# Attention, routed experts and a dense layer in one kernel: VectorE scans ahead of the masks, routing chains in turn, masks made on chip

## The chip, the cores and the metric

The kernel runs on one core of one Trainium2 chip. The metric is the device time of one execution in microseconds; the median of several runs counts. The engines are PE (TensorE), DVE (VectorE), ACT (ScalarE), POOL (GpSimd) and SP, which here only issues transfers.

## What is computed

The reference chains three parts. The shapes are batch 4, 8 heads, 768 steps, head dimension 48, so 3072 tokens of 384 numbers; 8 experts of width 1024; a dense layer of width 2048.

```python
for t in range(S):                                   # attention with decay
    state = alpha[:, :, t, :, None] * state + einsum('bhd,bhe->bhde', k[:, :, t], v[:, :, t])
    y[:, :, t] = einsum('bhd,bhde->bhe', q[:, :, t], state)
xn = x / (norm(x) + 1e-06)                           # routing, one expert per token
en = expert_emb / (norm(expert_emb) + 1e-06)
logits = xn @ en.T / tau
expert_idx = argmax(logits, axis=1)
gate_w = softmax(logits)[expert_idx]
out[mask_e] = gate_w * (maximum(x[mask_e] @ w1[e], 0) @ w2[e])
h = x @ w_in                                         # dense layer
out = where(h > 0, h, exp(minimum(h, 0)) - 1) @ w_out
```

## The kernel before

**Attention** works on 24 tiles of 128 tokens: 6 chunks of time (`cc`), and in each the 4 batch entries, whose state goes from chunk to chunk. `stR` and `stA` are DVE scans over the decays of a tile (`at`): R (L341) and its reciprocal (L342) scale the keys, A (L351) the queries; the products Kh (L344) and Qh (L353) are made on POOL. On PE, `stS` (L381) multiplies Qh by Kh into `psS`; `stP` (L388, DVE, two halves) multiplies that by a triangular mask from `cs` into P; `stC_values` (L426) multiplies P by the values; `stC_state` (L408) adds the part of the old state, from the second chunk on; `stD` (L464) turns a finished tile around and gives its eight logits, which DVE sums into `lg` (L469). `stT` makes the transposed keys and `stC_values` also the new state (U, L434). Three PSUM banks (`psG`) are used in turn: two for the halves of `psS`, one for U. The four `at` and four `qk` buffers are used in turn, with loads issued four tiles ahead on SP. The heads have 48 rows, laid at partitions 0 to 47 and 64 to 111; the rows between them are zeros that the loads of the first four tiles bring along.

The loop in `fast()` runs all engines by the order in which the code stands: pass `i` issues S of tile `i+1`, the scans of tile `i+2`, P of tile `i+1` and then D of tile `i-1` and the values of tile `i`. On DVE a pass is R(i+2), reciprocal, P(i+1) first half, A(i+2), P(i+1) second half, `lg`, then whatever the list `todo` holds.

`todo` is the **routing** of a group of tiles (groups of 6, 6, 4, 4, 2 and 2; the last ones are routed behind the loop). When the group's last tile is `j`, pass `j+2` appends `stR1` (an argmax chain over `lg` and a chain, `inv_norm`, for the norms of the tokens; the second one is a Newton iteration where each step needs the one before), `step` takes up to 12 operations from the list in a pass, pass `j+3` puts `stR2` (the positions of the tokens) ahead of what is left, and pass `j+4` ends the chain and releases the gates. Tokens are then written to DRAM sorted by expert (`put`, with a one-element POOL memset `tick` at L583 ahead of its indirect store). Expert weights come 12 pieces at a time from pass `WAIT-2` on, and each piece is split into a high part on ACT and a low part `wlo` on DVE (L204).

Before the loop the constants `cs` (identity, triangular mask, tables), the embeddings `emb_t` and the selector `rhsX` are loaded; 20 matmuls on `ones16` (`warm`, L285) run on PE, then 4 more behind S of tile 0. The eight embedding rows are normed by a chain of 14 small ACT operations (`inv_norm1`, L140 to L148) that begins and ends with a DVE reciprocal (L732), scaled on ACT (L733, L734), and transposed on PE (`eT`, L762) into the last columns of `rhsX`.

**moe1** goes through the eight experts with three matmuls per product (high by high, high by low, low by high). Beside it `decode` unpacks the dense layer's weights, and the rows of the next expert are loaded (`load_x`) and transposed (`turn`). At its end, `split_x` makes the high and low parts `xh`, `xl` (L1106, L1107) of the first 512 tokens of the dense layer, between the three copies of the last expert's result (L1041, L1042, L1045).

**moe2** has 6 blocks of 512 tokens with 16 steps each: 96 times `mm1` (L1187, nine matmuls into one PSUM bank) and, three steps behind, `mm2` (L1208 to L1210). The result of `mm1` goes through `mn` (L1189, DVE), an exponential (ACT), `g` (L1193, DVE), `gh` (ACT) and `gl` (L1197, DVE); `g` is the last reader of the bank. `mm1` has four banks of its own (`psH2`). In the first block the dense weights are split on the way (`split_dense`, L259 and L260).

Of the kernel before, what the change touches and what calls it, by code (L numbers as in the profile page):

```python
# [22 lines left out]
NT = NC * B  # L23
# [17 lines left out]
WAIT = 10  # L41
# [18 lines left out]
CONST = [("ident", 128), ("tri", 128), ("dec", E), ("base", E), ("tok", NT), ("key", E), ("cap", E), ("iota", E)]  # L60
# [3 lines left out]
def fused_kernel(ctx, tc, qk, a, v, emb, w12, wi, wo, cst, sel, cols, out):  # L64
# [12 lines left out]
    c = {}  # L77
# [25 lines left out]
    ss = const.tile([128, NT], F32, name="ss")  # L103
    tick = const.tile([1, 1], F32, name="tick")
# [23 lines left out]

    def inv_norm1(pool, x):

        shape = [x.shape[0], 1]
        y = pool.tile(shape, F32, name="rs_y1")
        t = pool.tile(shape, F32, name="rs_t1")
        h = pool.tile(shape, F32, name="rs_h1")
        yi, vec, act = y.bitcast(I32), nc.vector, nc.scalar
        first = [
            lambda: vec.tensor_scalar(yi, x.bitcast(I32), 1, None, op0=ALU.logical_shift_right),
            lambda: vec.tensor_scalar(yi, yi, -1.0, float(0x5F3759DF), op0=ALU.mult, op1=ALU.add),
        ]
        steps = [lambda: act.activation(out=h, in_=x, func=AF.Copy, scale=-0.5)]  # L140
        for _ in range(3):
            steps += [
                lambda: act.activation(out=t, in_=y, func=AF.Copy, scale=h),
                lambda: act.activation(out=t, in_=t, func=AF.Copy, scale=y),
                lambda: act.activation(out=t, in_=t, func=AF.Copy, bias=1.5),
                lambda: act.activation(out=y, in_=t, func=AF.Copy, scale=y),
            ]
        steps += [lambda: act.activation(out=y, in_=y, func=AF.Copy, scale=x, bias=1e-6)]  # L148
        return y, first, steps
# [137 lines left out]
    def attention():  # L287
        with ExitStack() as st:
# [27 lines left out]
            def load(i):  # L316
                if i >= NT:
                    return
                cc, b = divmod(i, B)
                at[i], qkt[i] = ats[i % LB], qks[i % LB]  # L320
                for t, src in ((at[i], a), (qkt[i], qk)):
                    for r in [slice(0, C2)] if i < LB else [slice(0, D), slice(HP, C2)]:
                        nc.sync.dma_start(out=t[r], in_=src[cc, r, b])
# [171 lines left out]
            def stR1(g):  # L495
# [168 lines left out]
            def fast():  # L664
                warm_t = sm.tile([128, 1], F32, bufs=1, name="warm_t")
                emb_t = sm.tile([E, 2 * NP * HP + 1], F32, bufs=1, name="emb_t")
# [10 lines left out]
                nc.vector.memset(ones16, 1.0)  # L677
# [5 lines left out]
                for t in G:  # L683
                    nc.gpsimd.memset(t, 0.0)
# [3 lines left out]
                nc.gpsimd.memset(zero, 0.0)  # L688
# [4 lines left out]
                for j in range(2):  # L693
# [3 lines left out]
                    if j == 0:  # L697
                        stE(j)
                        nc.scalar.activation(out=esq, in_=rows, func=AF.Square, accum_out=es)
# [3 lines left out]
                for f in guess:  # L703
                    f()
# [632 lines left out]
```

## Time and profile before

| what | us |
|---|---|
| median of 3 runs (790.78 to 794.12) | 793.1 |
| profiled execution | 795.59 |
| its span | 793.8 |
| attention in the span | 0 to 157 |
| moe1 | 157 to 385.5 |
| moe2 | 386.4 to 793.8 |
| PE busy in the span | 770.1 (97%) |
| DVE busy | 522.2 (66%) |
| ACT busy | 362.6 (46%) |
| POOL busy | 188.9 (24%) |

The stages were told apart by the first and the last matmul of each. The profiled execution is the one whose trace is read below; what lies outside its span is 1.8 us. The mean granted clock of PE over the span is 0.992 of full speed. In a timeline row the first number is the start and the second the duration; a number in square brackets is how long the engine stood idle just before, and behind the arrow is what it was waiting for. A row that ends in x4 is four operations in a row, and its duration runs from the first start to the last end.

### The profile page before, as it was taken

The numbers are of one execution on the slowest core, as the hardware profiler recorded it, in microseconds if no ns is written. First come the engines' busy times: TensorE is split into PE (matmuls) and PEld (weight loads), VectorE is DVE, ScalarE is ACT, GpSimd is POOL, SyncE is SP. The second block draws the span as 40 slices with busy tenths as digits, with TensorE's granted clock in tenths as the row PEclk, the third lists the DMA queues.
The fourth block names the chain that finished last, engine by engine and source line by source line (L and its number), as shares of the span: only waits on it lengthen the run. The fifth ranks groups of instructions, "written<-read, shape, count | busy, mean of one in ns | idle before, by whom it ended". The sixth has DMA issues, their size and how long they took to land.

```text
span 793.8 us, 13698 instructions
## 1 busy us (share of the span) xinstructions
PE 770.1 (97%) x5077; PEld 699.1 (88%) x5077; DVE 522.2 (66%) x1001; ACT 362.6 (46%) x802; POOL 188.9 (24%) x222
## 2 busy tenths in 40 slices
PE   7999998899999999999999999999999999999996
PEld 4888887489999999999898899999999999999996
DVE  6789999846877877896576755454555545545442
ACT  4667877435455455554545433333333323323231
POOL 5545667322333433342000020020002002002002
PEclk9899999999999999999999999999999999999999
DMA  9998773366665666661000010010001001001001
GB/s 245 245 259 205 233 202 92 109 176 201 185 198 184 204 198 204 213 200 35 1 1 1 1 40 1 0 40 1 1 1 40 1 1 40 1 0 41 1 1 40
DMA packets 44804, 76.25 MB, mean 96 GB/s; under 512 B 11958, under 2 KB 21302, under 8 KB 44734
## 3 DMA queue, kind: packets, MB, share of 16 engines
q1 hardware_dynamic: 41662, 65.89, 29.5%
q0 software_dynamic: 3072, 9.45, 3.3%
q8 instruction: 40, 0.66, 0.4%
q14 instruction: 30, 0.25, 0.1%
HBM read 63.12 MB, written 12.22 MB: 95 GB/s over the span
## 4 chain that ended last, share of the span: by engine, by line
PE 40%; issue 30%; DVE 3%; POOL 3%; ACT 2%; POOLq 0%; ACTq 0%
PE h L1187 6%; PE y L1031 5%; PE y L1033 4%; PE y L1032 4%; PE h L1000 4%; PE h L1001 4%; PE h L999 4%; POOL out_dram L1221 2%; PE o L1210 2%; PE o L1208 2%; PE o L1209 2%; PE t L980 1%; DVE dlo L260 1%; DVE g L1193 1%; DVE mn L1189 1%
## 5 line engine op out<-in xcount | busy, mean ns | idle before, releaser
L1189 DVE TENSOR_SCALAR mn<-h 128x512 f32<-128x512 f32 x96 | 66.2, 690 | 139.7 <-PE h L1187 139.7
L1190 ACT ACTIVATE mn<-mn 128x512 f32<-128x512 f32 x96 | 60.7, 632 | 171.7 <-DVE mn L1189 163.2
L1210 PE MATMUL o<-dwo,gl 128*128 128x384 f32 x384 | 129.4, 337 | 1.4 <-DVE gl L1197 1.4
L1209 PE MATMUL o<-dlo,gh 128*128 128x384 f32 x384 | 128.4, 334 | 0.0
L1208 PE MATMUL o<-dwo,gh 128*128 128x384 f32 x384 | 128.2, 334 | 0.0
L1187 PE MATMUL h<-xh,dwi 128*128 128x512 f32 x288 | 112.8, 392 | 0.6 <-ACT x2T L1045 0.6
L1187 PE MATMUL h<-xh,dlo 128*128 128x512 f32 x288 | 113.2, 393 | 0.0
L1187 PE MATMUL h<-xl,dwi 128*128 128x512 f32 x288 | 112.5, 392 | 0.0
L1221 POOL DMA_INDIRECT out_dram<-ob,ids x24 | 23.2, 965 | 340.8 <-ACT ob L1218 337.1
L1196 ACT ACTIVATE gh<-g 128x512 fp32r<-128x512 f32 x96 | 60.7, 633 | 77.9 <-DVE g L1193 77.9
L1003 ACT ACTIVATE hh<-h 128x432 fp32r<-128x432 f32 (+6 forms) x64 | 32.4, 506 | 107.1 <-PE h L1001 98.9
L204 DVE TENSOR_TENSOR wlo<-raw,whi 128x512 fp32r<-128x512 f32 x96 | 72.8, 786 | 5.6 <-ACT whi L201 5.6
L1193 DVE SCALAR_TENSOR_TENSOR g<-mn,h 128x512 f32<-128x512 f32 x96 | 66.1, 688 | 15.2 <-ACT mn L1190 14.7
L1208 PEld LDWEIGHTS o<-dwo,gh 128*128 128x128 f32 x384 | 72.0, 187 | 4.2
L1209 PEld LDWEIGHTS o<-dlo,gh 128*128 128x128 f32 x384 | 72.0, 187 | 4.0
L1210 PEld LDWEIGHTS o<-dwo,gl 128*128 128x128 f32 x384 | 72.2, 188 | 2.1 <-DVE gl L1197 1.7
L1004 DVE SCALAR_TENSOR_TENSOR hl<-h,hh 128x432 fp32r<-128x432 f32 (+6 forms) x64 | 36.7, 574 | 48.8 <-ACT hh L1003 47.4
L1031 PE MATMUL y<-hh,whi 128*128 128x432 f32 (+6 forms) x192 | 68.3, 356 | 0.0
L999 PE MATMUL h<-xh,whi 128*128 128x432 f32 (+6 forms) x192 | 66.5, 346 | 0.7 <-ACTq L1058 0.7
L244 POOL TENSOR_SCALAR dg<-dg 128x384 f32<-128x384 f32 x32 | 41.7, 1304 | 106.3 <-ACT dg L243 106.1
L1197 DVE TENSOR_TENSOR gl<-g,gh 128x512 fp32r<-128x512 f32 x96 | 65.7, 684 | 1.2 <-ACT gh L1196 1.1
L1001 PE MATMUL h<-xh,wlo 128*128 128x432 f32 (+6 forms) x192 | 66.4, 346 | 0.0
(217 smaller groups left out, 1508.9 us busy)
## 6 DMA issues: line engine op xcount, KB each, us to landing
raw<-in_w_dram SPq DMA_DIRECT2D x96, 256.0 KB
qk<-in_qk_dram SPq DMA_DIRECT2D x40, 192.0 KB
raw<-in_wi_dram SPq DMA_DIRECT2D x16, 384.0 KB
raw<-in_wo_dram SPq DMA_DIRECT2D x16, 384.0 KB
vt<-in_v_dram SPq DMA_DIRECT2D x24, 192.0 KB
xr<-xs SPq DMA_DIRECT2D x7, 576.0 KB
at<-in_alpha_dram SPq DMA_DIRECT2D x40, 99.0 KB
xs<-zero SPq DMA_DIRECT2D x7, 288.8 KB
```

The source lines that it names most:

```text
L204: nc.vector.tensor_tensor(l[:, sl], r, h[:, sl].bitcast(F32), op=ALU.subtract)
L999: nc.tensor.matmul(ps, wh, xh[:, kk], start=(kk == 0), stop=False)
L1001: nc.tensor.matmul(ps, wl, xh[:, kk], start=False, stop=(kk == KD - 1))
L1031: nc.tensor.matmul(acc[e][d], wh, hh, start=(f == 0), stop=False)
L1187: nc.tensor.matmul(ps, l, x, start=(n == 0), stop=(n == len(terms) - 1))
L1189: nc.vector.tensor_scalar(mn, ps, 0.0, None, op0=ALU.min)
L1190: nc.scalar.activation(out=mn, in_=mn, func=AF.Exp)
L1193: nc.vector.scalar_tensor_tensor(g, mn, -1.0, ps, op0=ALU.add, op1=ALU.max)
L1197: low.append(lambda: nc.vector.tensor_tensor(gl, g, gh.bitcast(F32), op=ALU.subtract))
L1208: nc.tensor.matmul(o_, gh[:, sl], wh, start=(f == 0), stop=False)
L1209: nc.tensor.matmul(o_, gh[:, sl], wl, start=False, stop=False)
L1210: nc.tensor.matmul(o_, gl[:, sl], wh, start=False, stop=(f == M - 1))
```

## The change

**Start.** The embeddings come within `cs`, unscaled and already in the layout of `rhsX`, so the loads of `emb_t` and `rhsX` and the chain `inv_norm1` with its scaling and its transposes are gone. Identity and triangular mask are made by POOL (`affine_select`) in a tile `masks`; `cs` has 97 columns where it had 320. The zero rows of the first four `qk` tiles are set by DVE and POOL instead of loaded, and the order of the loads is another one; the load of the lower rows waits for the setting. The memsets of G and `zero` on POOL go behind Qh of tile 1. `warm` runs 6 instead of 4 behind S of tile 0, and 3 at the end of pass 0. The norm of the embeddings is a matmul with ones in pass 2 and 17 DVE operations in passes 5 to 7, and one more operation of the routing chain multiplies the logits by it (another is joined to its neighbour, so the count stays).

**DVE order.** `stA` goes ahead of both halves of `stP` in every pass. The two chains of `stR1` alternate one by one, `stR2` alternates with what is left, 16 operations are taken in a pass instead of 12, and a group ends one pass earlier. `WAIT` is 9.

**moe1.** The rows of expert 1 are loaded ahead of two loads of the dense weights, `decode` runs by another schedule of about the same length, and the first `split_x` moves ahead of the last `mm2`.

**moe2.** `mm1` uses the three banks of `psG`, which moe1 used, instead of four of its own, and the special order of terms in the first step is gone.

```diff
-WAIT = 10
+WAIT = 9
...
-CONST = [("ident", 128), ("tri", 128), ("dec", E), ("base", E), ("tok", NT), ("key", E), ("cap", E), ("iota", E)]
+CONST = [("emb", NP * E), ("dec", E), ("base", E), ("tok", NT), ("key", E), ("cap", E), ("iota", E), ("tau", 1)]
...
+            def load_k(i, apart=False):
...
+                for n in [slice(1, 2), slice(0, 1)] if apart else [slice(0, 2)]:
+                    for r in [slice(HP, C2), slice(0, D)]:
+                        nc.sync.dma_start(out=t[r, n], in_=qk[cc, r, b, n])
...
                 ops = [
+                    lambda: nc.vector.tensor_tensor(l, l, en.to_broadcast(s3), op=ALU.mult),
                     lambda: nc.vector.tensor_reduce(mx, l, axis=AX.X, op=ALU.max),
-                    lambda: nc.vector.tensor_tensor(e_, l, mx.to_broadcast(s3), op=ALU.is_equal),
                     lambda: nc.vector.tensor_tensor(l, l, mx.to_broadcast(s3), op=ALU.subtract),
-                    lambda: nc.vector.tensor_tensor(e_, e_, c["dec"][:, None, :].to_broadcast(s3), op=ALU.mult),
+                    lambda: nc.vector.scalar_tensor_tensor(e_, l, 0.0, c["dec"][:, None, :].to_broadcast(s3), op0=ALU.is_ge, op1=ALU.mult),
...
-                load(0)
+                nc.vector.memset(qks[0][lanes, 1], 0.0)
+                nc.vector.memset(ones16, 1.0)
+                nc.vector.memset(qks[0][lanes, 0], 0.0)
+                nc.gpsimd.memset(c["ident"], 0.0)
+                nc.gpsimd.affine_select(out=c["ident"], in_=c["ident"], compare_op=ALU.not_equal, fill=1.0, base=0, pattern=[[-1, 128]], channel_multiplier=1)
+                nc.gpsimd.memset(c["tri"], 1.0)
+                nc.gpsimd.affine_select(out=c["tri"], in_=c["tri"], compare_op=ALU.is_ge, fill=0.0, base=0, pattern=[[1, 128]], channel_multiplier=-1)
+                nc.vector.memset(qks[1][lanes], 0.0)
+                nc.gpsimd.memset(qks[2][lanes], 0.0)
+                nc.gpsimd.memset(qks[3][lanes], 0.0)
+                load(0, True)
+                load(1)
+                load_a(2)
+                load_v(0)
+                load_k(2)
                 nc.sync.dma_start(out=cs, in_=cst)
-                nc.sync.dma_start(out=emb_t, in_=emb)
-                load(1)
-                load_v(0)
-                load(2)
-                nc.sync.dma_start(out=rhsX, in_=sel[:, None, :].to_broadcast([128, NP, CW + E]))
                 load_v(1)
                 load(3)
                 load_v(2)
...
                     stR(i + 2)
+                    stA(i + 2)
                     stP(i + 1, 0)
-                    if i == 0:
-                        nc.vector.reciprocal(en, en)
-                        nc.scalar.activation(out=rows, in_=rows, func=AF.Copy, scale=en)
-                        nc.scalar.activation(out=rows, in_=rows, func=AF.Copy, scale=rtau)
-                    stA(i + 2)
                     stP(i + 1, 1)
...
-                        todo[:0] = stR2(last[i - 3])
+                        todo[:] = in_turn(stR2(last[i - 3]), todo)
...
-                        m, n = stR1(last[i - 2])
-                        k = len(m) // 2
-                        todo.extend([f for x in zip(m[::2], m[1::2], n[:k]) for f in x] + n[k:])
+                        todo.extend(in_turn(*stR1(last[i - 2])))
...
-                    step(5)
+                    step(8 if i < 7 else 16)
                     for f in lag:
                         f()
                     lag.clear()
-                    step(7)
...
-                    for g in [g for j, g in last.items() if i == j + 4]:
+                    for g in [g for j, g in last.items() if i == j + 3]:
...
+            def in_turn(*chains):
+
+                return [x[n] for n in range(max(map(len, chains))) for x in chains if n < len(x)]
...
+                    if n == len(blocks):
...
+                        for kk in range(KD):
+                            split_x(x2T, *first, 0, kk)
                     if n >= LAG:
                         mm2(*blocks[n - LAG])
...
-                    j = (n - 2) * 4 // 7
+                    j = (n - 4) * 3 // 5
...
-                ps = psH.tile([128, U], F32, name="h2")
+                ps = psG.tile([128, U], F32, tag="g", name="h2")
```

DVE behind the first scans, where S of tile 0 has been multiplied: first as it stands in the kernel before, then as it stands now (`rs_y` is the result of the embeddings' norm chain on ACT).

```order
L388 TENSOR_TENSOR P<-psS,cs 128x512 x2
L341 SCALAR_TENSOR_TENSOR R<-at_124,pz 112x528
L342 RECIPROCAL at_124<-R 112x4
L388 TENSOR_TENSOR P<-psS,cs 128x512
L732 RECIPROCAL rs_y_202<-rs_y_202 8x1
L351 SCALAR_TENSOR_TENSOR A<-at_124,pz 112x528
L388 TENSOR_TENSOR P<-psS,cs 128x512
L341 SCALAR_TENSOR_TENSOR R<-at_125,pz 112x528
```

```order
L381 TENSOR_TENSOR P<-psS,masks 128x512 x2
L334 SCALAR_TENSOR_TENSOR R<-at_126,pz 112x528
L335 RECIPROCAL at_126<-R 112x4
L344 SCALAR_TENSOR_TENSOR A<-at_126,pz 112x528
L381 TENSOR_TENSOR P<-psS,masks 128x512 x2
L334 SCALAR_TENSOR_TENSOR R<-at_127,pz 112x528
```

The scan A of tile 2 no longer stands behind the reciprocal of the embeddings' norm, nor behind P of tile 1.

DVE in the second of the passes that route group 0, from P up to the next scan R; before, then now (L561 to L563 and L554 to L556 are `stR2`, L118 to L124 and L120 to L127 the norm chain).

```order
L388 TENSOR_TENSOR P<-psS,cs 128x512
L561 TENSOR_TENSOR t<-psR,oh 128x48
L562 TENSOR_REDUCE pos<-t 128x6
L563 TENSOR_SCALAR pos_i<-pos 128x6
L120 SCALAR_TENSOR_TENSOR rs_y<-rs_t,rs_y 128x6
L118 SCALAR_TENSOR_TENSOR rs_t<-rs_y,ss 128x6
L119 TENSOR_TENSOR rs_t<-rs_t,rs_y 128x6
L120 SCALAR_TENSOR_TENSOR rs_y<-rs_t,rs_y 128x6
L118 SCALAR_TENSOR_TENSOR rs_t<-rs_y,ss 128x6
L119 TENSOR_TENSOR rs_t<-rs_t,rs_y 128x6
L120 SCALAR_TENSOR_TENSOR rs_y<-rs_t,rs_y 128x6
L123 TENSOR_TENSOR rs_y<-rs_y,ss 128x6
```

```order
L381 TENSOR_TENSOR P<-psS,masks 128x512 x2
L554 TENSOR_TENSOR t<-psR,oh 128x48
L122 SCALAR_TENSOR_TENSOR rs_y<-rs_t,rs_y 128x6
L555 TENSOR_REDUCE pos<-t 128x6
L120 SCALAR_TENSOR_TENSOR rs_t<-rs_y,ss 128x6
L556 TENSOR_SCALAR pos_i<-pos 128x6
L121 TENSOR_TENSOR rs_t<-rs_t,rs_y 128x6
L122 SCALAR_TENSOR_TENSOR rs_y<-rs_t,rs_y 128x6
L125 TENSOR_TENSOR rs_y<-rs_y,ss 128x6
L126 TENSOR_SCALAR rs_y<-rs_y 128x6
L127 RECIPROCAL rs_y<-rs_y 128x6
L511 TENSOR_TENSOR lg<-lg,rs_y 128x48
```

The three operations of `stR2` now alternate with the norm chain, which ends in this pass.

ACT from the end of moe1 into moe2; before, then now (L1041, L1045 and L1038, L1040 copy the last expert's result, L1106 and L1103 are the high parts of the first 512 tokens).

```order
L1041 ACTIVATE x2T<-y_7921 128x368
L1106 ACTIVATE xh_8126<-x2T 128x512
L1045 ISA
L1045 ACTIVATE x2T<-y_7923 128x368
L1106 ACTIVATE xh_8127<-x2T 128x512
L1106 ACTIVATE xh_8128<-x2T 128x512
L259 ACTIVATE dwi<-wd 128x384
```

```order
L1103 ACTIVATE xh_8117<-x2T 128x512
L1103 ACTIVATE xh_8118<-x2T 128x512
L1103 ACTIVATE xh_8119<-x2T 128x512
L1035 TENSOR_LOAD off_i
L1035 ISA x2
L1038 ISA
L1038 ACTIVATE x2T<-y_7946 128x368
```

The three high parts go from between and behind the last copies to ahead of them.

## Rows read from the trace of the kernel before

**Rows 1.** Windows: stretch, length, busy PE, PEld, DVE, ACT, POOL; granted clock, DMA share, GB/s
```profile
15.00:20.00 5.00, 2.76 (x22) 2.45 (x23) 3.40 (x6) 2.54 (x7) 2.56 (x2) 0.72 1.08 234
20.00:25.00 5.00, 5.00 (x50) 4.76 (x50) 3.53 (x5) 2.48 (x7) 2.56 (x2) 0.59 1.04 225
35.00:127.00 92.00, 89.22 (x1304) 78.88 (x1300) 84.04 (x190) 68.59 (x217) 53.61 (x54) 1.00 0.78 211
127.00:157.00 30.00, 24.29 (x211) 17.15 (x211) 26.52 (x146) 16.12 (x53) 15.23 (x28) 0.94 0.35 107
200.00:370.00 170.00, 170.00 (x944) 165.16 (x943) 138.13 (x231) 88.66 (x179) 64.38 (x56) 1.00 0.60 189
```

**Rows 2.** Timeline of PE, 8 to 30 us: start, us, line, operation, idle before it
```profile
9.98 1.03 PE L285 MATMUL warm<-ones 128*128 128x512 bf16 x4
...
14.15 0.61 PE L434 MATMUL psU<-vt,Kt 128*64 128x48 f32 x16
16.71 0.41 PE L762 MATMUL eT<-cs,emb_t 8*128 8x8 f32 x4 [1.95 <-ACT emb_t L734]
17.65 2.08 PE L381 MATMUL psS<-Qh,Kh 48*128 48x128 f32 x16 [0.53 <-POOL Qh L353]
...
24.61 1.16 PE L381 MATMUL psS<-Qh,Kh 48*128 48x128 f32 x16
...
29.07 1.16 PE L381 MATMUL psS<-Qh,Kh 48*128 48x128 f32 x16 [0.41 <-POOL Qh L353]
```

**Rows 3.** Timeline of DVE, 10 to 18 us
```profile
14.90 0.15 DVE L732 RECIPROCAL rs_y<-rs_y 8x1 f32<-8x1 f32 x1 [1.42 <-ACT rs_y L148]
```

**Rows 4.** DMA issues from 0 to 12 us: KB each
```profile
qk<-in_qk_dram SPq DMA_DIRECT2D x4, 448.0 KB
...
rhsX<-in_sel_dram SPq DMA_DIRECT2D x1, 208.0 KB
...
cs<-in_cst_dram SPq DMA_DIRECT2D x1, 160.0 KB
```

**Rows 5.** Timeline of POOL, 0 to 7 us
```profile
0.83 1.05 POOL L684 MEMSET G<- 112x256 f32 x4 [0.38 <-POOLq L1325]
...
5.87 1.28 POOL L344 TENSOR_TENSOR Kh<-qk,R 112x512 f32<-112x512 f32 x1 [3.42 <-DMA qk<-in_qk_dram]
```

**Rows 6.** Page, costliest groups: a POOL operation, mean ns of one
```profile
L244 POOL TENSOR_SCALAR dg<-dg 128x384 f32<-128x384 f32 x32 | 41.7, 1304 | 106.3 <-ACT dg L243 106.1
```

**Rows 7.** Timeline of DVE in a plain tile, 45.3 to 51 us
```profile
45.38 0.69 DVE L388 TENSOR_TENSOR P<-psS,cs 128x512 f32<-128x512 f32 x1 [1.43 <-PE psS L381]
45.99 1.24 DVE L351 TENSOR_TENSOR_SCAN A<-at,pz 112x528 f32<-112x528 f32 x1
...
47.83 1.24 DVE L341 TENSOR_TENSOR_SCAN R<-at,pz 112x528 f32<-112x528 f32 x1
...
50.72 0.69 DVE L388 TENSOR_TENSOR P<-psS,cs 128x512 f32<-128x512 f32 x1 [1.43 <-PE psS L381]
```

**Rows 8.** Timeline of DVE in two routing tiles, 50.7 to 63 us
```profile
54.03 0.21 DVE L510 TENSOR_TENSOR lg<-lg,mx 128x48 f32<-128x48 f32 x1
54.15 0.20 DVE L511 TENSOR_TENSOR e__829<-e__829,cs 128x48 f32<-128x48 f32 x1
...
60.09 0.17 DVE L118 SCALAR_TENSOR_TENSOR rs_t<-rs_y,ss 128x6 f32<-128x6 f32 x1
60.30 0.17 DVE L119 TENSOR_TENSOR rs_t<-rs_t,rs_y 128x6 f32<-128x6 f32 x1
```

**Rows 9.** Timeline of PE, 93 to 102 us
```profile
100.00 1.16 PE L381 MATMUL psS<-Qh,Kh 48*128 48x128 f32 x16 [1.26 <-POOL tick L583]
```

**Rows 10.** Timeline of PE at the start of moe2, 386 to 388 us
```profile
386.39 0.50 PE L1187 MATMUL h<-xh,dwi 128*128 128x512 f32 x1 [0.59 <-ACT x2T L1045]
```

**Rows 11.** Timelines of DVE and PE in moe2, 429.5 to 432.5 us
```profile
430.17 0.69 DVE L1193 SCALAR_TENSOR_TENSOR g<-mn,h 128x512 f32<-128x512 f32 x1 [0.16 <-ACT mn L1190]
...
431.91 0.39 PE L1187 MATMUL h<-xh,dwi 128*128 128x512 f32 x1
```

More of the change, by code (lines that the diff above doesn't have):

```diff
@@ L127, in inv_norm @@
         return y, steps
[L129 to L149, printed above, removed]
     wq = [(e, s) for e in range(E) for s in range(FB * FW // SLOT)]
@@ L687, in fast @@
                 zero = xp.tile([128, 1, XW], F32, tag="xt", name="zero")
-                nc.gpsimd.memset(zero, 0.0)
-                rows, rtau = emb_t[:, :2 * NP * HP], emb_t[:, 2 * NP * HP:]
-                es = sm.tile([E, 1], F32, name="es")
-                esq = wk.tile([E, 2 * NP * HP], BF16, bufs=1, tag="junk", name="esq")
-                en, guess, newton = inv_norm1(sm, es)
                 for j in range(2):
@@ L696, in fast @@
                     stH(j)
-                    if j == 0:
-                        stE(j)
-                        nc.scalar.activation(out=esq, in_=rows, func=AF.Square, accum_out=es)
+                    stE(j)
+                for t in G:
+                    nc.gpsimd.memset(t, 0.0)
+                nc.gpsimd.memset(zero, 0.0)
+                nc.gpsimd.memset(ones_f, 1.0)
                 stS(0)
                 stT(0)
-                warm(ps1, "psY", 4)
-                for f in guess:
-                    f()
-                nc.vector.reciprocal(rtau, rtau)
-                stE(1)
+                warm(ps1, "psY", 6)
+                for h2 in range(2):
+                    nc.scalar.activation(out=rhsX[:, :, h2 * D:(h2 + 1) * D],
+                                         in_=c["ident"][:, None, h2 * HP:h2 * HP + D].to_broadcast([128, NP, D]), func=AF.Copy)
                 stP(0, 0)
                 stP(0, 1)
-                for f in newton:
-                    f()
+                inv, norms = inv_norm(sm, es)
+                norms += [
+                    lambda: nc.vector.reciprocal(c["tau"], c["tau"]),
+                    lambda: nc.vector.tensor_tensor(en[:, 0], inv, c["tau"].to_broadcast([128, E]), op=ALU.mult),
+                ]
                 lag = []
@@ L759, in fast @@
                     if i == 0:
-                        eT = psD.tile([128, NP, E], F32, tag="psX", name="eT")
-                        for p in range(NP):
-                            nc.tensor.transpose(eT[:, p], rows[:, p * 128:(p + 1) * 128], c["ident"][:E, :E])
-                        nc.scalar.activation(out=rhsX[:, :, CW:CW + E], in_=eT, func=AF.Copy)
+                        warm(psD, "psX", 3)
+                        nc.scalar.activation(out=rhsX[:, :, CW:CW + E], in_=c["emb"].rearrange("p (n e) -> p n e", n=NP), func=AF.Copy)
+                    if i == 2:
+                        nc.scalar.activation(out=esq, in_=rhsX[:, :, CW:CW + E], func=AF.Square)
+                        nc.tensor.matmul(pz[:, 64:64 + NP * E], ones_f, esq.rearrange("p n e -> p (n e)"), start=True, stop=True)
+                        sums = pz[:, 64:64 + NP * E].rearrange("p (n e) -> p e n", n=NP)
                     if i == 3:
@@ L1084, in moe1 @@
                             turn(e + 1, f - 4)
+                    if n == len(blocks):
+                        for nm in ("xh2", "xl2"):
+                            first.append([stage.tile([128, U], F32R, tag="raw", name=nm) for _ in range(KD)])
+                        for kk in range(KD):
+                            split_x(x2T, *first, 0, kk)
                     if n >= LAG:
```

75 lines of the change are left out of this document (34 added, 41 removed).

## The prediction

> **What bounds the kernel now.** I read the busy times by stage first, then PE's timeline where PE stands idle, then the engine that each wait names. In the table by stage, moe1 has PE busy for all of 170.00 us and the main part of attention for 89.22 of 92.00 [rows 1]. So nothing can be won in these stages but idle PE time, and there are three places with some.
>
> The first is the start. PE ends U of tile 0 at 14.15 + 0.61 = 14.76 us and begins S of tile 2 at 17.65 [rows 2]. In these 2.9 us it waits 1.95 us for the scaled embeddings and 0.53 us for Qh of tile 2; Qh is late because the scan A stands behind a DVE reciprocal that waits 1.42 us for the small ACT operations of the embeddings' norm [rows 3]. Right behind, the granted clock is 0.72 and then 0.59 on average [rows 1]: PE runs for some time at 1.2 instead of 2.4 GHz, S of tile 2 takes 2.08 us where that of tile 3 takes 1.16, and from S to S are 6.96 us where the next tile needs 4.46 [rows 2]. In that next tile 0.41 us are a wait for Qh again, and it stands once more in the tile behind.
>
> The second place is the loop. From P to P are 50.72 - 45.38 = 5.34 us, in which DVE waits 1.43 us for S [rows 7]: in a plain tile PE is the bound. The 2.78 us that PE idles in this window are waits of S behind routing passes, the largest 1.26 us [rows 9].
>
> The third is the step into moe2, where PE waits 0.59 us for the copies of the last expert [rows 10].
>
> **The change, part by part.**
>
> *Start, the wait.* With the embeddings' chain gone, PE goes from U to S of tile 2 through three warm matmuls. Four take 1.03 us [rows 2], so three take 0.8, and S could begin at 15.5. What could hold it is Qh: A of tile 2 now follows R at once, without the wait of 1.42 us [rows 3] and half a P of 0.69 ahead of it: 2.1 us earlier, so that Qh, too, lets S begin at about 15.5. Against that, `ones16` is set behind a memset of 32x512 on DVE, for which no row stands; the 128x512 product of 0.69 us [rows 7] is the nearest and the upper end, zero the lower. The two more warm matmuls behind S of tile 0 cost 0.5 at most. I take S of tile 2 at 15.6, a gain of 2.0 us, between 0.9 and 2.3.
>
> *Start, the clock.* Before the slow stretch PE stood idle for 1.95 and 0.53 us. These two waits are what goes away, and PE has work without a long break. The tile then takes what the next one takes: 6.96 - 4.46 = 2.5 us, or nothing if the clock falls all the same.
>
> *Start, Qh.* S of tiles 4 and 5 each wait 0.41 us [rows 2]. Before, S, half of P, A and Qh form a chain: 1.16 + 0.61 + 1.24 + 1.28 = 4.29 us from S to S [rows 2, 5, 7], just above the 4.05 us of PE's own work in these tiles. With A ahead of P the chain is cut, and 0.8 us go. In sum the start gives 5.3 us.
>
> *What the start needs in return.* The loads: 208 KB of selector, 223 of 320 columns of the 160 KB and 16 of 112 rows of four times 448 KB, in all 575 KB, are loaded no more [rows 4], 2.5 us at the 230 GB/s that the full DMA engines move there [rows 1]. On POOL the first product begins at 5.87, when its data has landed [rows 5]. New ahead of it are two memsets of 32x1024, two of 128 columns and two `affine_select`. By the memsets of G, 1.05 us for 1024 columns [rows 5], the memsets take 2.4 us. For `affine_select` there is no row: as fast as a memset it would take 0.13 us, by the 1.304 us of a 128x384 operation [rows 6] 0.43. From 0.83 us on that makes 3.5 to 4.1 us, and the small memsets of the value tiles 0.3 more: POOL is free about when R of tile 0 ends. The memsets of G and `zero` come later, where POOL waits for R of tile 2. I put all of this at nothing; SP's new waits for memsets end before the transfers ahead of them land.
>
> *Loop.* Before, S of the next tile could come no earlier than 4.29 us behind S, which is 1.05 under the tile's 5.34; a routing pass adds 12 operations at 0.12 to 0.21 us [rows 8], 1.4 to 2.5 us on DVE, and overdraws that. Now R and A of tile i+2 wait only for P of tile i. From S of tile i: 1.16, then P, P and `lg` (47.83 - 45.38 - 1.24 = 1.2), R, reciprocal and A (2.6), Qh (1.28), in sum 6.25 us against two tiles, 10.68. The slack grows from 1.05 to 4.4 us, an estimate from these rows. DVE's 84.04 us of work [rows 1] fit into PE's 89.22. A pass now takes 16 operations; those that need nothing of each other start every 0.12 us and those of one chain every 0.21 [rows 8]. That makes 1.9 to 3.4 us, inside the slack. The 17 operations for the embeddings (at 0.21 us 3.6 us over three passes) are inside it too, as are the weight pieces, which only come a pass earlier. I take 2.5 of the 2.78 us, between 0 and 2.78.
>
> *End of attention.* From 127 to 157 PE idles 30.00 - 24.29 = 5.7 us [rows 1], in chains that the change touches little. Nothing, between a loss of 0.5 and a gain of 1.0.
>
> *moe1.* PE has no idle time; loads and `decode` move beside it: nothing.
>
> *Step into moe2.* The first 512 tokens are split before the last `mm2`, so the first matmul no longer stands behind the last expert's copies; the wait of 0.59 us goes [rows 10], and so do the short waits for single parts just behind it: 0.8 us, between 0.6 and 1.2. The three banks instead of four: `mm1` must now wait for `g` three steps back. In the tightest place `g` ends at 430.17 + 0.69 = 430.86, and the matmul that needs its bank starts at 431.91 [rows 11]: 1.05 us to spare, nothing.
>
> Sum: 5.3 + 2.5 + 0.8 = 8.6 us. The profiled execution's 795.59 would become 787.0; it lies 2.5 above the median of 793.1, so the forecast against the median is **784.5 us**.
>
> **The rivals.**
>
> *Loads bound the start.* The DMA engines are full through these stretches [rows 1]. If PE in tiles 2 to 6 comes to wait for data, only the 575 KB count: 2.5 + 2.5 + 0.8 = 5.8 us, 787.3. For it speaks the full DMA share, against it that no wait of this stretch names a load.
>
> *The clock falls anyway*, for instance behind a new wait near 15 us: 2.5 us less, 787.0. PE's first matmuls are tied to a memset that now comes later.
>
> *Routing gains nothing.* The operations in turn cost the full 0.21 us each, so two passes with 16 and 11 add 5.7 us, less 2.9 of waiting in them, and the low parts of two weight pieces (0.69 us each, by the operation of the same size in [rows 7]) 1.4: 4.2 us, at the edge of the slack of 4.4. If it is overdrawn, S waits as before, 2.5 us less, 787.0. The rows speak against it, 0.12 against 0.21 [rows 8].
> The Trainium skill, "VectorE: DVE Perf Modes", section "The DRAIN you can't avoid", says that the next DVE operation starts only when the pipe of the one before is empty and that chaining without semaphores saves nothing, by which alternating chains would be worth nothing. By this rule the time would be this rival's; the trace's 0.12 does not agree with it for operations that are independent.
>
> *Two of these together*, or a start that keeps its wait for another reason: about 3.3 us left, 789.8, no change that can be told.
>
> *Slower: POOL's first work.* Kh of tile 0 stands behind two `affine_select`, whose price no row shows, and a load of tile 2 waits on SP for the memset behind them, with all later loads queued on SP. POOL is free at about 4.3 and needed at 5; each us beyond delays S of tile 0 by a us. The gain is eaten when the two take 9.3 us more than I take, and 8 us for each would give 793.1 - 8.6 + 14.5 = 799. The nearest rows (0.13, 0.43) are far from that.
>
> **How the numbers follow.** The forecast has 0.43, loads 0.16, clock 0.11, routing 0.11, two of them 0.12, slower 0.07. A measurement of this kernel can tell about 0.5% from no change, 4.0 us. The first four cases lie below 789.1: faster 0.81, same 0.12, slower 0.07. The range: all upper ends give 2.3 + 2.5 + 0.8 + 2.8 + 1.2 + 1.0 = 10.6 us, 782.5, and the runs before spread by up to 2.3 us from the median, so 780.3; on the other side the case of two together, 789.8, is held.
>
> **What would show it.** In the trace after: S of tile 2 near 15.6 and S of tile 4 near 23.7 us instead of 29.07 [rows 2], clock at 1.00 from 15 to 25 us, no idle time of PE that ends on Qh or `tick` in the loop, DVE steps of 0.12 us in the routing passes, the first `mn` of moe2 about a us sooner relative to the last y, and no wait of `mm1` for `g`. I would be wrong if PE waits for a load in the first eight tiles, if POOL begins Kh of tile 0 well behind 5 us, or if a wait at another place takes up the 5 us that attention gains.

## The result, and the profile after

The changed kernel takes 786.05 us (median of 5 runs, 784.83 to 786.79) against 793.1 before (5 runs, 790.78 to 797.6): ratio 0.9906, interval 0.9887 to 0.9924, so 6 to 9 us less. The forecast was 784.5, the range 780.3 to 789.8. The profiled execution took 785.51 us with a span of 783.8: 10.0 us of span less than the one before. That is more than the 7.05 us by which the medians differ, and the reason turns out to be part of the answer.

Where the 10.0 us are is read from the starts of PE's matmuls in both traces; the same boundaries serve for the experiments. "Start" ends with S of tile 6; the step from tile 2 to 3 within it is where the clock was low before. "Loop" is S of tile 6 to S of tile 22, "tail" from there to the last values matmul, "to moe1" from the last values matmul to the first expert matmul, "step" from the last y of moe1 to the first matmul of moe2.

| kernel | S6 at | of it tile 2 to 3 | loop | tail | to moe1 | moe1 | step | moe2 |
|---|---|---|---|---|---|---|---|---|
| before | 38.85 | 6.96 | 88.21 | 14.48 | 18.77 | 225.15 | 0.92 | 400.22 |
| changed | 35.34 | 4.38 | 84.65 | 12.91 | 17.85 | 225.11 | 0.17 | 400.59 |
| difference | -3.5 | -2.6 | -3.6 | -1.6 | -0.9 | 0 | -0.75 | +0.4 |

The table of windows of the changed kernel has the clock at 1.00 throughout, where [rows 1] had 0.72 and 0.59, and PE without a gap in the loop (columns as in [rows 1]):

```profile
15.00:20.00 5.00, 4.92 (x75) 4.03 (x72) 3.72 (x6) 2.49 (x7) 3.15 (x4) 1.00 1.03 197
20.00:25.00 5.00, 4.44 (x74) 3.96 (x69) 4.13 (x7) 3.08 (x12) 3.19 (x3) 1.00 1.07 195
25.00:30.00 5.00, 4.39 (x62) 4.00 (x63) 4.11 (x7) 3.62 (x14) 2.62 (x3) 1.00 1.05 225
30.00:120.00 90.00, 90.00 (x1324) 80.06 (x1324) 85.02 (x212) 70.73 (x224) 57.95 (x60) 1.00 0.95 243
```

In the start some idle time is left, though. PE's timeline after, the rows that answer to [rows 2]:

```profile
12.33 1.16 PE L374 MATMUL psS<-Qh,Kh 48*128 48x128 f32 x16 [1.28 <-POOL Qh L346]
...
15.43 0.82 PE L265 MATMUL warm<-ones 128*128 128x512 bf16 x3
16.34 1.16 PE L374 MATMUL psS<-Qh,Kh 48*128 48x128 f32 x16
...
20.71 1.16 PE L374 MATMUL psS<-Qh,Kh 48*128 48x128 f32 x16 [0.32 <-POOL Qh L346]
...
25.23 0.41 PE L761 MATMUL pz<-esq,ones_f 128*128 128x32 f32 x2 [0.47 <-ACT esq L760]
25.57 1.16 PE L374 MATMUL psS<-Qh,Kh 48*128 48x128 f32 x16
...
30.00 1.16 PE L374 MATMUL psS<-Qh,Kh 48*128 48x128 f32 x16 [0.39 <-POOL Qh L346]
```

These are S of tiles 1 to 5. Tile 2 begins at 16.34, and 2.6 us of the gain are the step behind it, now at full clock. But tile 1 comes later than before (12.33 instead of 11.60), and tiles 4 and 5 wait for the new norm matmul and for what stands behind it. Two waits of DVE stand ahead of S of tiles 3 and 5:

```profile
16.22 1.25 DVE L334 TENSOR_TENSOR_SCAN R<-at,pz 112x528 f32<-112x528 f32 x1 [1.12 <-DMA at<-in_alpha_dram]
...
25.73 1.25 DVE L334 TENSOR_TENSOR_SCAN R<-at,pz 112x528 f32<-112x528 f32 x1 [1.44 <-PE pz L761]
```

R of tile 3 waits for its load; R of tile 5 waits for the norm matmul, which writes the PSUM tile `pz` that R reads. S of tile 4 stands right behind that matmul on PE, which itself waits 0.47 us for the squares (`esq`).

### The profile page after: what moved, and what is told of

Same layout as the page of the kernel before. It is cut to its first block, busy times and chain, and to the rows that moved or that the text cites. A ratio compares the mean times of both kernels' runs of the same rounds, so it can differ in the third digit from the quotient of the medians.

```text
span 783.8 us, 13738 instructions
## 1 busy us (share of the span) xinstructions
PE 764.5 (98%) x5080; PEld 694.8 (89%) x5080; DVE 521.9 (67%) x1017; ACT 358.1 (46%) x787; POOL 192.2 (25%) x229
## 4 chain that ended last, share of the span: by engine, by line
PE 38%; issue 31%; DVE 5%; POOL 3%; ACT 2%; DMA 0%; POOLq 0%; SPq 0%; ACTq 0%; DVEq 0%
PE h L1181 6%; PE y L1031 4%; PE y L1032 4%; PE y L1033 4%; PE h L1000 4%; PE h L1001 4%; PE h L999 4%; POOL out_dram L1215 2%; PE o L1204 2%; PE o L1202 2%; PE o L1203 2%; DVE dlo L240 1%; PE t L980 1%; DVE g L1187 1%; DVE mn L1183 1%
## 5 line engine op out<-in xcount | busy, mean ns | idle before, releaser
L1032 PE MATMUL y<-hl,whi 128*128 128x432 f32 (+6 forms) x192 | 66.3, 345 | 0.2 <-DVE hl L1004 0.2
```

The costliest lines, as they stand in the source:

```text
L1032: nc.tensor.matmul(acc[e][d], wh, hl, start=False, stop=False)
```

## The experiments

All ratios are to the kernel before, runs taken on the same chip in turn. Stage lengths of each trace stand in a table behind the experiments.

**scan_first.** One edit to the kernel before:

```diff
                     stR(i + 2)
+                    stA(i + 2)
                     stP(i + 1, 0)
...
-                    stA(i + 2)
                     stP(i + 1, 1)
```

> The kernel before with one edit: A of tile i+2 stands ahead of both halves of P on DVE; routing as before. If the order of the scan is what frees the loop, the waits of S for Qh and tick between tiles 6 and 22 (2.8 us before) fall to under 0.5 us, and the two waits of 0.41 us at tiles 4 and 5 go too: 3 to 4 us less in all. If the alternating chains are what frees it, the loop keeps at least 2 of its 2.8 us and under 1.5 us are won.

788.61 us, ratio 0.9916 (0.9881 to 0.9951). The loop is 84.66 us long, as in the changed kernel, and PE's table of waits for it is empty. Tiles 4 and 5 follow at 3.98 us each. So the place of one scan alone gives the whole gain of the loop.

**in_turn.** The other edit of the loop alone:

```diff
-                        todo[:0] = stR2(last[i - 3])
+                        todo[:] = in_turn(stR2(last[i - 3]), todo)
...
+                        todo.extend(in_turn(*stR1(last[i - 2])))
...
-                    step(5)
+                    step(8 if i < 7 else 16)
...
-WAIT = 10
+WAIT = 9
```

> The kernel before with the other edit alone: routing chains one by one in turn, 16 operations a pass, a group ended a pass earlier, WAIT 9; A stays between the halves of P. If the scan's place sets the loop, S still waits behind the first routing passes, by up to 1 us more where 16 operations stand now in place of 12: between 0.5 us faster and 1.5 slower. If the chains set it, 2 us or more are won in the loop.

792.83 us, ratio 0.9991 (0.9969 to 1.0013): no change that can be told. PE keeps waiting for POOL in the loop; the waits of PE in this kernel, and for comparison in the one before (engine, what waited, for what: us in total, times, longest):

```profile
PE psS L381 <- POOL tick L583: 1.4, 3, 0.7
PE psS L381 <- POOL Qh L353: 0.5, 1, 0.5
```

```profile
PE psS L381 <- POOL tick L583: 2.0, 3, 1.3
PE psS L381 <- POOL Qh L353: 0.4, 1, 0.4
```

The longest wait is shorter, 0.7 instead of 1.3, and the loop 86.97 us instead of 88.21, of which 0.5 also differs between traces of the unchanged loop (87.72 to 88.21). What the scan's place does to POOL shows in POOL's waits in the loop, before and then in the changed kernel (in scan_first, with the scan's place alone, they are 3.4 us in 15 waits, the longest 0.3):

```profile
POOL Qh L353 <- DVE A L351: 14.1, 13, 2.2
```

```profile
POOL Qh L346 <- DVE A L344: 2.7, 12, 0.2
```

**loop_both.** Both edits, old start, old moe1 and moe2.

> The kernel before with both edits of the loop, without anything of the new start, moe1 or moe2. By the trace after, the loop from tile 6 to the last S gains 3.5 us; with the 0.8 us at tiles 4 and 5 and up to 0.5 at tile 2 (A ahead of the reciprocal) 4 to 5 us. If the loop's gain needs the new start (earlier loads, data in time), 2 us or less. The clock's slow stretch behind tile 1 should stay, since the wait for the embeddings stays.

787.33 us, ratio 0.9903 (0.9871 to 0.9936). The loop is 84.66: the routing chains add nothing to what the scan does alone. The step from tile 2 to 3 took 7.08 us here, the clock fell as before. This kernel has none of the new start, and its median is within 1.3 us of that of the changed one, which was not measured beside it.

**warm_gap.** The kernel before with matmuls in PE's idle time:

```diff
                     if i == 0:
+                        warm(psD, "psX", 8)
                         eT = psD.tile([128, NP, E], F32, tag="psX", name="eT")
```

> The kernel before with eight more warm matmuls in pass 0, ahead of the transposes of the embeddings, where PE stands idle for 1.95 us. If the idle time is why the clock falls, the granted clock stays at 1.00 from 15 to 25 us, S of tile 2 begins within 0.5 us of 17.65 and S of tile 3 follows it by about 4.4 instead of 6.96 us: 2.5 us less in that place. If the clock falls for another reason, the step from tile 2 to 3 stays near 7 us.

791.21 us, ratio 0.9957 (0.9939 to 0.9975). S of tile 2 is no earlier than in the trace before, the granted clock is 1.00 from 15 to 25 us, and 2.25 us are won by tile 3, and kept:

```profile
14.72 1.90 PE L285 MATMUL warm<-ones 128*128 128x512 bf16 x8
16.97 0.41 PE L763 MATMUL eT<-cs,emb_t 8*128 8x8 f32 x4 [0.35 <-ACT emb_t L734]
17.90 1.16 PE L381 MATMUL psS<-Qh,Kh 48*128 48x128 f32 x16 [0.52 <-POOL Qh L353]
...
22.36 1.16 PE L381 MATMUL psS<-Qh,Kh 48*128 48x128 f32 x16 [0.41 <-POOL Qh L353]
```

In the six other traces in which PE stands idle ahead of the transposes, the clock falls in five and not in the sixth. The idle time there is 1.83, 1.95, 1.97, 2.01 and 2.13 us (loop_both, before, scan_first, in_turn, banks_only), the step from tile 2 to 3 behind it 7.08, 6.96, 5.58, 5.59 and 5.57. In split_early, where nothing in the start was changed, the idle time is 1.55, the step 4.46, and the clock stays at 1.00:

```profile
16.37 0.41 PE L762 MATMUL eT<-cs,emb_t 8*128 8x8 f32 x4 [1.55 <-ACT emb_t L734]
17.30 1.16 PE L381 MATMUL psS<-Qh,Kh 48*128 48x128 f32 x16 [0.52 <-POOL Qh L353]
...
21.75 1.16 PE L381 MATMUL psS<-Qh,Kh 48*128 48x128 f32 x16 [0.41 <-POOL Qh L353]
```

The length of the idle time does not order the steps: among the five, the longest has the shortest step. Nor does it tell which execution falls, since split_early waits 1.55 and 0.52 us ahead of S of tile 2, 2.07 in all, and scan_first and loop_both, which fell, wait only 1.97 and 1.83. What is shown is that the clock did not fall in the two traces in which matmuls fill the wait, and that the cost differs from one execution to the next: 0 to 2.5 us with the old loop (6.96 against 4.46), 3.1 in loop_both against loop_fill below (7.08 against 3.98).

How much of it a median holds can be read from the mean granted clock that is listed for each run. Of the 43 runs of the kernel before that were taken beside the experiments, five have 0.997 or more; they took 791.01 to 791.34 us. The ten runs of warm_gap took 790.71 to 792.83, and their median, 791.21, is the same as that of these five.

**split_early.** The kernel before with `split_x` ahead of the last `mm2`; the four banks stay.

> The kernel before with the first split of the dense layer's tokens ahead of the last mm2; mm1 keeps its four banks. If this move is what the step into moe2 gains, the first mm1 starts 0.8 to 1.1 us earlier relative to the last y. After, 0.67 of 1.07 us were lost again at the end of the first block, where PE waited 1.63 instead of 1.37 us for gl. If that is DVE's own backlog, it happens here too and 0.3 to 0.5 us stay; if it comes from the three banks, 1 us stays.

795.42 us, ratio 1.0015 (0.9995 to 1.0036). The median says little: four of the ten runs took 791.86 to 792.92 us at a mean clock of 0.998 or more, six took 795.0 to 796.34 at 0.991 to 0.994, so runs of one kernel lie 3 us apart with the clock. In the trace, which is of one of the four, both theories missed: the first `mm1` comes 1.78 us behind the last y, 0.86 later than before. It waits for the last copy of moe1, which now stands behind the splits on ACT:

```profile
382.81 0.50 PE L1184 MATMUL h<-xh,dwi 128*128 128x512 f32 x1 [1.46 <-ACT x2T L1040]
```

**banks_only.** The kernel before with `mm1` of moe2 on `psG`:

```diff
-                ps = psH.tile([128, U], F32, name="h2")
+                ps = psG.tile([128, U], F32, tag="g", name="h2")
...
```

The rest of the edit keeps `psG` open through moe2.

> The kernel before with mm1 of moe2 on the three banks of psG and nothing else. With the split moved alone the first mm1 came 1.78 us behind the last y instead of 0.92, waiting for the last copy of the last expert. If it is the new banks that hold the first mm1 (they are those from which the copies read), the three shared banks take that wait off: 0.92 falls to 0.5 or less, and it waits for the split of the tokens instead. If the banks don't matter, 0.92 stays. The length of moe2 from the first mm1 to the last matmul stays within 0.5 us of 400.2 if three banks are enough.

One run, 792.74 us, so only its trace is used. The step is 0.55 us and now waits for the split itself:

```profile
383.22 0.50 PE L1186 MATMUL h<-xh,dwi 128*128 128x512 f32 x1 [0.23 <-ACT xh L1106]
```

With banks of its own the first `mm1` waits for the copies that empty moe1's y, also when the split is done (split_early); with those of `psG` it does not. The bank is one half of the step's gain, the split the other, and the split without the bank is a loss. With both (the changed kernel) the step is 0.17 us. From the last y to the last matmul of moe2 it is 401.14 us before, 401.13 in banks_only, 401.87 in split_early and 400.75 in the changed kernel: only both together gain at the end, 0.4 us. Of the 0.75 us, the rest is lost again at the end of moe2's first block, where PE waits for `gl`; before, in the changed kernel, in split_early and in banks_only:

```profile
430.07 0.45 PE L1210 MATMUL o<-dwo,gl 128*128 128x384 f32 x1 [1.37 <-DVE gl L1197]
```

```profile
420.03 0.44 PE L1204 MATMUL o<-dwo,gl 128*128 128x384 f32 x1 [1.63 <-DVE gl L1191]
```

```profile
426.37 0.44 PE L1207 MATMUL o<-dwo,gl 128*128 128x384 f32 x1 [1.30 <-DVE gl L1194]
```

```profile
427.26 0.44 PE L1209 MATMUL o<-dwo,gl 128*128 128x384 f32 x1 [1.46 <-DVE gl L1196]
```

It is longer in the two kernels with three banks (1.46, 1.63); moe2 as a whole, from its first `mm1`, is 400.51 to 400.59 us in the seven traces with three banks and 400.09 to 400.22 in the seven with four. Whether the banks or the earlier start of `mm1` cause the longer wait is not shown; no matmul of `mm1` waits for a bank in the changed kernel.

**whole_rows.** The changed kernel with the first four qk tiles loaded whole:

```diff
-                for n in [slice(1, 2), slice(0, 1)] if apart else [slice(0, 2)]:
-                    for r in [slice(HP, C2), slice(0, D)]:
-                        nc.sync.dma_start(out=t[r, n], in_=qk[cc, r, b, n])
+                for r in [slice(0, C2)] if i < LB else [slice(HP, C2), slice(0, D)]:
+                    nc.sync.dma_start(out=t[r], in_=qk[cc, r, b])
...
```

The memsets of their zero rows are gone with it.

> The changed kernel with one part undone: the first four qk tiles are loaded whole, 448 KB each in one piece, the zero rows with them, and the memsets of those rows are gone. If the bytes count, 256 KB more cost 1.1 us at 230 GB/s: S of tile 1 at 13.0 or later (12.33 in the changed kernel), the total 0.5 to 1.5 us longer. If pieces of 48 rows move more slowly than whole ones (193 to 224 GB/s from 5 to 15 us after, 277 to 284 before), the rate is back above 260 GB/s there and S of tile 1 comes at 12.4 or earlier, the total within 0.5 us of the changed kernel or below it.

788.09 us, ratio 0.9941 (0.9920 to 0.9963), where the changed kernel had 0.9906; the expected total, that of the changed kernel or less, was missed. Of the six runs two took 785.75 and 785.76 us, the latter the profiled one, and four 787.63 to 789.03 at nearly the same mean clock (0.994 to 0.997); no trace shows what these pay. In the trace S of tile 1 comes at 11.37 and S of tile 6 at 33.99, 1.35 us earlier than in the changed kernel, but the loop is 1.0 us longer. The rates from 5 to 15 us, the changed kernel and then whole_rows (last columns: clock, DMA share, GB/s):

```profile
5.00:10.00 5.00, 4.95 (x36) 2.69 (x34) 4.30 (x7) 0.22 (x1) 2.79 (x3) 1.00 1.05 224
10.00:15.00 5.00, 3.72 (x47) 2.70 (x46) 4.83 (x7) 1.80 (x6) 5.00 (x9) 1.00 1.08 193
```

```profile
5.00:10.00 5.00, 4.36 (x34) 2.54 (x33) 4.81 (x7) 0.57 (x3) 3.69 (x3) 1.00 1.04 273
10.00:15.00 5.00, 4.75 (x61) 3.28 (x58) 4.83 (x8) 2.42 (x8) 5.00 (x10) 1.00 1.06 244
```

With the DMA engines equally full, the kernel that loads the first four tiles in pieces of 48 rows moves 224 and 193 GB/s here, the one that loads them whole 273 and 244 (before: 277 and 284). The bytes that the change saves are lost again in the rate. That the size of the pieces sets the rate is not shown: from the fifth tile on every kernel loads qk in pieces of 48 rows, and from 30 to 120 us the changed kernel moves 243 GB/s at a DMA share of 0.95. What sets S of tile 1 stays open as well: in whole_norm, with whole tiles too, it comes at 12.43.

**norm_early.** The changed kernel with the square and the matmul of the embeddings' norm in pass 0:

```diff
-                    if i == 2:
                         nc.scalar.activation(out=esq, in_=rhsX[:, :, CW:CW + E], func=AF.Square)
                         nc.tensor.matmul(pz[:, 64:64 + NP * E], ones_f, ...
```

> The changed kernel with one piece moved: the square and the matmul for the embeddings' norm stand in pass 0, not in pass 2. If they are what delays tiles 4 and 5 (the matmul waits 0.47 us for the square, R waits 1.44 us for the matmul), the steps of S from tile 3 to 4 and from 4 to 5 go from 4.86 and 4.44 us to about 4.05 each, 1.2 us less, at a cost of 0.3 at most at tile 2. If the loads are the limit there, the steps stay above 4.3 and under 0.5 us is won.

786.6 us, ratio 0.9924 (0.9895 to 0.9954). The steps are 4.45 and 4.18 us instead of 4.86 and 4.44, so 0.67 us less, about half of what was expected; a wait of 0.40 us for Qh stays at tile 4. The loop is 85.61, and the total as in the changed kernel.

**norm_at3.** The same with the decays of tile 3 loaded earlier (`load_a(3)` ahead of `cs`).

> As norm_early, and the decays of tile 3 are loaded ahead of the constants and of the values of tile 1. R of tile 3 waits 1.12 us for them in the changed kernel, and S of tile 3 comes 0.32 us late. If that load's place is the reason, the step of S from tile 2 to 3 goes from 4.38 to 4.05 us and 0.3 us more is won than in norm_early. If the DMA engines as a whole are the limit, another load is late in its place and nothing more is won.

786.97 us, ratio 0.9922 (0.9896 to 0.9949). The step from tile 2 to 3 stays at 4.38, so the load's place is not its reason; the next two are 3.98 and 4.00. S of tile 6 comes at 33.96, but the loop takes 86.11 us and the tail 14.47: the clock fell there (0.69 from 128 to 132 us).

**loop_fill.** loop_both with the eight warm matmuls of warm_gap.

> The kernel before with both edits of the loop and eight warm matmuls in pass 0 ahead of the transposes of the embeddings; the old start otherwise, old moe1 and moe2. If the new start is worth no more than what it saves at the clock, this kernel has S of tile 6 at 34.8 us or earlier (35.34 in the changed kernel, 37.41 with the loop's edits alone, where the clock fell), the loop at 84.7 us, and takes 0 to 1 us more than the changed kernel, which also gains about 1 us ahead of moe1 and 0.4 us in the step into moe2. If the removed loads and the embeddings' chain count by themselves, it is 2 us or more behind the changed kernel.

787.68 us, ratio 0.9916 (0.9899 to 0.9932), 1.9 us behind the changed kernel measured beside it (785.8, see after_again), between the two cases that were expected; the trace decides. S of tile 6 comes at 34.42, earlier than in the changed kernel: the new start is worth no more than the clock it saves. The distance lies behind it: a loop of 85.80, a tail of 14.48 with the clock fallen (0.73 from 128 to 132 us), 0.5 us to moe1, and the old step into moe2.

**whole_norm and after_again.** whole_rows and norm_early together, and the changed kernel once more beside it.

> The changed kernel with whole_rows and norm_early together. S of tile 6 came at 33.99 with the first; the second took 0.7 us off tiles 3 to 6. If both add, S of tile 6 comes at 33.0 to 33.4 us, 2 us earlier than in the changed kernel. The whole is 1 to 2 us faster than the changed kernel of the same call if the loop keeps its 84.65 us, and the same if it lengthens by 1 us as it did in both single edits (85.65 and 85.61).

> The changed kernel once more, on the same chip as the two kernels beside it. Loop 84.7 us and S of tile 6 within 0.5 us of 35.3 if its first trace is typical. In none of the loads or waits is anything drawn by lot but the clock: it stays at 1.00 up to 35 us; behind tile 22 it may fall as it did in norm_at3, then 1.57 us longer there.

784.27 us (783.75 to 785.62), ratio 0.9879 (0.9862 to 0.9895), against 785.8 us (784.61 to 786.2), ratio 0.9893 (0.9877 to 0.991). The combined version is 1.5 us faster by the medians, with intervals that overlap. The changed kernel repeats its first trace in the main (S of tile 6 at 35.61, loop 84.65, clock at 1.00 in the tail); but S of tile 1 comes 0.35 us later, and the step from tile 3 to 4 takes 5.31 us instead of 4.86 and the next 3.98 instead of 4.43, so not only the clock differs between executions. In the combined version's trace the waits of tiles 4 and 5 are gone and the loop keeps its 84.65 us:

```profile
16.58 1.16 PE L373 MATMUL psS<-Qh,Kh 48*128 48x128 f32 x16
20.96 1.16 PE L373 MATMUL psS<-Qh,Kh 48*128 48x128 f32 x16 [0.33 <-POOL Qh L345]
24.94 1.16 PE L373 MATMUL psS<-Qh,Kh 48*128 48x128 f32 x16
28.94 1.16 PE L373 MATMUL psS<-Qh,Kh 48*128 48x128 f32 x16
```

| kernel | S6 at | of it tile 2 to 3 | loop | tail | to moe1 | step | moe2 |
|---|---|---|---|---|---|---|---|
| scan_first | 36.16 | 5.58 | 84.66 | 14.48 | 18.07 | 0.92 | 400.20 |
| in_turn | 37.74 | 5.59 | 86.97 | 12.91 | 18.40 | 0.92 | 400.19 |
| loop_both | 37.41 | 7.08 | 84.66 | 12.91 | 18.35 | 0.92 | 400.19 |
| warm_gap | 36.61 | 4.45 | 87.72 | 14.47 | 17.90 | 0.92 | 400.20 |
| loop_fill | 34.42 | 3.98 | 85.80 | 14.48 | 18.33 | 0.92 | 400.22 |
| split_early | 36.00 | 4.46 | 88.17 | 12.91 | 18.79 | 1.78 | 400.09 |
| banks_only | 37.04 | 5.57 | 87.72 | 14.47 | 18.28 | 0.55 | 400.57 |
| whole_rows | 33.99 | 3.98 | 85.65 | 12.90 | 18.52 | 0.17 | 400.51 |
| norm_early | 35.02 | 4.37 | 85.61 | 12.90 | 18.87 | 0.17 | 400.52 |
| norm_at3 | 33.96 | 4.38 | 86.11 | 14.47 | 18.46 | 0.17 | 400.51 |
| whole_norm | 34.28 | 4.38 | 84.65 | 12.90 | 18.09 | 0.17 | 400.54 |
| after_again | 35.61 | 4.30 | 84.65 | 12.90 | 17.80 | 0.17 | 400.53 |

## Why the prediction was right, and where its steps were not

**Start, the wait** (2.0 us): 1.3. The embeddings' chain left the path, but S of tile 1 came 0.73 us later than before, since Kh waited 1.75 us for its qk tile (the last row of POOL below). So a wait for a load within the first eight tiles, which the prediction had named as a sign of being wrong, did occur. The rival of the loads was right that they are felt here, but it counted the saved bytes at a fixed 230 GB/s, and the rate was 193 to 224 while the first four tiles came.

**Start, the clock** (2.5): 2.6 in the pair of traces, and warm_gap shows that work for PE in the idle time saves it. The mistake is in how the term was carried to the median. It was counted in full, with a fixed 2.5 us between the trace and the median, though an unchanged start can also run without it (split_early). The 10.0 us of the traces hold 2.6 us here and 1.6 in the tail that an execution of the kernel before pays only sometimes. At a mean clock of 0.997 or more the kernel before took 791.01 to 791.34 us in five runs and the changed one 784.61 to 786.15 in six: about 5.6 us between their medians. What the medians of all runs differ by beyond that, 7.05 us at first and 8.56 in after_again, is put down to the clock. This split is an estimate, since not all of these runs were taken side by side.

**Start, Qh** (0.8): the step is right for the scan (3.98 and 3.98 us in scan_first), but nothing of it was left, because the new norm matmul took its place at tiles 4 and 5. The prediction asked whether the 17 DVE operations fit and left out the matmul and the shared `pz`. norm_early and whole_norm show that this was wrong.

**What the start needs in return** (nothing): POOL is free at about 4.2 us and Kh of tile 0 starts at 5.24, so the rival of the slow `affine_select` fell: each takes 0.29 us, between the two bounds.

```profile
1.18 0.29 POOL L667 TENSOR_SCALAR_AFFINE_SELECT masks<-masks 128x128 f32<-128x128 f32 x1
...
2.03 0.94 POOL L671 MEMSET qk<- 32x1024 f32 x1
...
5.24 1.28 POOL L337 TENSOR_TENSOR Kh<-qk,R 112x512 f32<-112x512 f32 x1 [1.02 <-DVE R L334]
...
9.76 1.29 POOL L337 TENSOR_TENSOR Kh<-qk,R 112x512 f32<-112x512 f32 x1 [1.75 <-DMA qk<-in_qk_dram]
```

**Loop** (2.5): 3.6, of which scan_first alone gives 3.55. The working named the right edit, by the chain of S, P, A and Qh. The term was too small because it counted PE's idle time in a window and not the length of the loop: within the loop PE was busy for 85.37 of 88.21 us before and for all of 84.65 after, so its busy time shrank by 0.7 as well. The rival that routing in turn gains nothing was half right: the operations do start in shorter steps, but behind the early scan that is worth nothing more that could be told. The steps in the changed kernel's DVE are 0.10 to 0.12 us, each shorter than the operation that it follows. The prediction weighed against this a rule of the Trainium skill, "VectorE: DVE Perf Modes", section "The DRAIN you can't avoid", by which the next operation starts only behind an empty pipe. The same paragraph adds that a next operation that is not held starts earlier, which the prediction left out, and so the rule as it used it does not fit these rows:

```profile
122.88 0.16 DVE L115 TENSOR_SCALAR rs_y<-ss 128x4 int32<-128x4 int32 x1
122.99 0.19 DVE L502 TENSOR_REDUCE mx<-lg 128x4 f32<-128x32 f32 x1
123.09 0.20 DVE L116 TENSOR_SCALAR rs_y<-rs_y 128x4 int32<-128x4 int32 x1
123.21 0.19 DVE L503 TENSOR_TENSOR lg<-lg,mx 128x32 f32<-128x32 f32 x1
```

**End of attention** (nothing): 2.5 us less in the traces. 1.57 of it is the clock in the tail (0.59 from 136 to 140 us before):

```profile
136.00:140.00 4.00, 4.00 (x44) 3.31 (x42) 3.07 (x15) 0.86 (x4) 1.21 (x4) 0.59 0.26 99
```

In the fourteen traces the tail is 14.47 or 14.48 six times and 12.90 or 12.91 eight times. The clock fell there in one of the six that carry the new start, and in five of the eight that don't; PE's waits ahead of it are the same in before and in the changed kernel (0.8 and 1.5 us), so what decides it stays open. The other 0.9 us lie between the tail and the first expert matmul, which ran from 17.80 to 18.87 us over the kernels without a pattern that I could assign to an edit; in the changed kernel PE waits 0.4 us for the gathered rows and before 1.2. That too stays open.

**Step into moe2** (0.8): 0.75 in place, 0.4 by the end; the first `mn` comes 0.43 us sooner relative to the last y, where about 1 was foreseen. The term was right in size and wrong in mechanism: the prediction took the split's place for the cause, but the bank holds the matmul as well. It also missed that PE waits for `gl` at the end of the block whatever comes ahead, and by more.

So the forecast came within 1.6 us of the median in part by luck. Its main mechanism, the scan's place in the loop, held, but the parts fit by errors in both directions: 1.8 us too much in the start, 1.1 too little in the loop, 2.5 in the traces at the end of attention that it put at nothing, and two clock terms of which a median holds only a part. (The lower end of its range is 0.1 off: 782.5 less 2.3 is 780.2.)

Open besides: the loop took 84.65 us in five of the traces with the early scan and 85.6 to 86.1 in four others (whole_rows, norm_early, norm_at3, loop_fill). About half of it, in loop_fill three quarters, stands in PE's timeline as two or three short waits each, 0.17 to 0.66 us, most of them for `yT` on ACT or P on DVE (0.48 of 1.0 us in whole_rows, 0.67 of 1.5 in norm_at3); what makes those late, and the rest, is not explained.

## What to carry to other kernels

When a scan or another long operation feeds the next tile and stands behind one that waits for this tile's matmul, the two make one chain from matmul to matmul; write down that chain's length against the tile's time before anything else, for moving one line was worth more here, by the medians, than all the rest (scan_first 4.9 us, the whole change 7.05). A term that comes from the clock in one trace belongs into the forecast with a share, not in full: look at the clock of all runs, and try whether a few filler matmuls in PE's idle time remove the low stretch. A small matmul that writes a PSUM tile from which a hot loop reads costs what the loop waits for it, even when its own time is 0.4 us: here 1.3 us at tiles 4 and 5 (steps of 4.86 and 4.44 us against 3.98 and 4.00 in whole_norm).

## What had not been expected of the hardware

From 5 to 15 us, with the DMA engines full in all of them, the changed kernel moved 193 to 224 GB/s, and whole_rows, which differs from it only in how the first four qk tiles and their zero rows come, 244 to 273. The granted clock of the same start differed from one execution to the next: behind PE's idle time at the end of pass 0 it fell in five traces and stayed at 1.00 in a sixth, and split_early's ten runs have mean clocks of 0.998 or more with 791.86 to 792.92 us, or 0.994 or less with 795.0 to 796.34. With that time filled by matmuls it stayed at 1.00 in both kernels that were tried.
